# Layer two's weight pairs: sums in two parts, later roundings of what is stored, an earlier plan, and reused x tiles

## The chip, the core and the metric

The kernel runs on one core of one Trainium2 chip. The time is the device time of one execution in microseconds (us), taken over several executions; the profile is one further execution. The engines that matter here: TensorE (PE) multiplies matrices, ScalarE (ACT) and VectorE (DVE) work elementwise, SyncE (SP) and GpSimd (POOL) issue the transfers (DMAs). Each engine goes through its own instructions strictly in their order in the program; between engines semaphores hold an instruction back until what it reads is there, or until the memory that it writes has been read out.

## What is computed

```python
def reference(q, k, v, moe_w_in, moe_w_out, moe_alpha, moe2_w_in, moe2_w_out):
    x = retention(q, k, v)            # decayed causal attention, 2304 tokens x 512
    h = x @ moe_w_in                  # layer one, 512 -> 2048
    x = (np.maximum(h, 0) + moe_alpha * np.minimum(h, 0)) @ moe_w_out
    h = x @ moe2_w_in                 # layer two, 512 -> 2048
    return (h / (1 + np.exp(-1.702 * h))) @ moe2_w_out
```

The lines above are a shortening of the reference. Weights arrive as 64-bit floats, whose words the kernel reads as pairs of 32-bit integers and turns into float32 itself.

## The kernel before, in words

It has three stretches: attention (to about 80 us), layer one (to about 490 us) and layer two (to the end). Every float32 product is made of three passes of PE over rounded halves: each operand is split into a rounded high half (`copy`, L85, on ACT) and the rest as a low half (`sub`, L88, on DVE).

**Layer one** is 80 steps. A step is a chunk of tokens (512 columns, in one chunk 256) and one of 16 blocks of 128 hidden units. `mm1` (L403) makes the hidden block in 12 matmuls; `activate` does two Relu on ACT (L413, L414) and one operation on DVE (L415); `split` makes the high half on ACT (L85, gsf<-g) and the low half on DVE (L88, gsf<-g,gsf); `mm2` (L446) multiplies these gsf halves with the second weight in 12 matmuls. PE runs `mm1` of step i and then `mm2` of step i-2. Steps 32 to 47 and 64 to 79 are 512 wide, steps 48 to 63 are 256 wide. In between, `x_split` (x<-xf) rounds the next chunk's inputs.

**Layer two** uses a scheme with seven products in place of eight, so its weights go through sums and differences of quarters. It runs as units of 12 or 6 matmuls (L567).

**The weight pairs of layer two** are the work that the change moves. There are eight pairs j of second weight rows. Each has two halves e. For one half: `w_load`/`w_piece` (L112, issued by POOL, two DMAs of 512 KB into a tile raw0 or raw1), `w_abs` (L116, ACT, into a tile cv), `w_clamp` (L120, L123, DVE), `w_top` (L130, DVE), `w_low` (L137, DVE, the last reader of the raw tile). For the pair then: `sums1` and `sums2` (four `add` each on DVE, L474); `r_store` (five DMAs of SP, L181 to L185: three quarters and the four sums of `sums1`, to rg in memory, needed later by layer two's first product); `b_hi` (L85, ACT, rounds a quarter or a sum in its own place, so it may only run once r_store has read that place out); `b_lo` (L200, DVE); `b_store` (L206, L208 or L211, SP, to sg in memory). Blocks 0, 3 and 6 are quarters of the converted words (cv), blocks 1, 2, 4 and 5 are sums.

**The order** is written by a plan: `pair_words` gives each action a time; `tick` turns a time into a place in the steps, and the main loop emits what is due after `mm1` and before `activate`, or after `mm2` and before `split`. A plan's time only sets the place in each engine's order; an instruction starts when its engine comes to it and its inputs are there. The plan's two first numbers are the times of the two halves' conversion, the next two those of their loads.

**The end of layer one**: `x2_load` (L504, SP) fetches layer one's result in two parts k = 0 and 1 into tiles xr, `x2_step` makes sums, high and low halves from them for layer two, `r_load` (L542, SP) fetches the first weights of layer two, `r_split` rounds them.

Of the kernel before, what the change touches and what calls it, by code (L numbers as in the profile page):

```python
# [7 lines left out]
F32 = mybir.dt.float32  # L8
# [21 lines left out]
R, RN = 3, 384  # L30
# [9 lines left out]
def kernel(  # L40
# [18 lines left out]
    def pool(name, bufs, **kw):  # L59
        return ctx.enter_context(tc.tile_pool(name=name, bufs=bufs, **kw))  # L60
# [4 lines left out]
    xp = (pool("xp", 1), pool("xq", 1))  # L65
# [27 lines left out]
    def at(time, fn, *args):  # L93
        events.append((time, len(events), fn, args))
# [118 lines left out]
    def pair_words(j, t0, t1, l0, l1, slots, home):  # L213
        for e, (t, ld) in enumerate(((t0, l0), (t1, l1))):
            key = 2, 2 * j + e
            at(tick(ld), w_load, key, w2, slots[e])
            at(tick(ld) + 0.01, w_piece, key, w2, 1)
            for fn, d in ((w_abs, 0.0), (w_clamp, 1.6), (w_top, 3.0), (w_low, 4.4)):
                at(tick(t + d), fn, key)
        t = t1 + 6.2  # L220
        at(tick(t), sums1, j, home)
        at(tick(t + 0.9), r_store, j)
        at(tick(t + 1.5), sums2, j)
        for g, blocks in enumerate(((0, 3), (6, 1), (2, 4, 5))):
            for i in blocks:
                at(tick(t + 1.8 + 2.4 * g), b_hi, j, i)
                at(tick(t + 4.2 + 2.4 * g), b_lo, j, i)
                at(tick(t + 5.4 + 2.4 * g), b_store, j, i)


    ld, r_t, k_t, s_t, sc_t, av_t, xs_t = {}, {}, {}, {}, {}, {}, {}
# [239 lines left out]
    xt2, g2, ws, rw, tm, bank, xr = {}, {}, {}, {}, {}, {}, {}  # L471
# [21 lines left out]
    def x2_load(r, k):  # L493
        for h in range(2):
            if r:
                t = cvp.tile([128, 2, RN], F32, tag="cv", name="xr", bufs=2)
            else:
                t = xp[0].tile([128, 2, RN], F32, tag=f"x{2 * k + h}", name="xr")
            xr[k, h] = t
            f = t.rearrange("p c n -> p (c n)")  # L500
            for c, (c0, c1) in enumerate(CH):
                s0, s1 = max(c0, r * 2 * RN), min(c1, r * 2 * RN + 2 * RN)
                if s0 < s1:
                    nc.sync.dma_start(  # L504
                        out=f[:, s0 - r * 2 * RN:s1 - r * 2 * RN],
                        in_=x1[c][:, 2 * h + k, s0 - c0:s1 - c0],
                    )
# [22 lines left out]
    def x2_steps(k, t, step, gap):  # L530
        for i in range(7):
            for phase in range(3):
                at(t + step * i + gap * phase, x2_step, k, i, phase)
# [153 lines left out]
    for m, t in enumerate(pace):  # L687
        d = 0.75 if m < 3 else 0.5
# [12 lines left out]
    with tc.manual_schedule():  # L701
# [47 lines left out]
        n1 = base + n_s  # L749
        homes = {c: xp[c] for c in range(2)}  # L750
        for n, (_, c, m0, _) in enumerate(BLOCKS[N_FIRST:], 1):
            homes[c] = xp[n % 2]
            for k in range(NK):
                t = starts[c, m0] - (4 if n == 1 else 4.4) + 0.9 * k
# [8 lines left out]
        def tick(us):  # L763
            for begin, length in PAUSES:
                us += length if us >= begin else 0
            i = max(n for n in range(n_s) if begins[n] <= us)
            return base + i + (us - begins[i]) / (begins[i + 1] - begins[i])

        for j, plan in enumerate((
# [4 lines left out]
        )):  # L774
            pair_words(j, *plan)
        for k in range(2):
            at(n1 - 5.6 + 3.0 * k, x2_load, 0, k)
            x2_steps(k, n1 - 4.6 + 2.8 * k, 0.35, 0.5)
        for n in range(3):
            at(n1 - 1.5, r_load, n)  # L780
        for n in range(2):
# [24 lines left out]
        for r in range(R):  # L806
# [18 lines left out]
            if r + 1 < R:  # L825
                for n in range(3):
                    at(z + 2 * NU - 9.2, r_load, n)
                for k in range(2):
                    at(z + NU + 1 + 23 * k, x2_load, r + 1, k)
                    x2_steps(k, z + NU + 5.2 + 23 * k, 2.8, 0.9)  # L830
# [84 lines left out]
```

## Time and profile before

| | before |
|---|---|
| median of 3 runs | 846.1 us (845.58 to 847.55) |
| the profiled execution | 845.46 us |
| its span on the core | 843.7 us |
| mean granted TensorE clock | 0.993 of full speed |
| PE busy | 826.7 us, 98% of the span |
| DVE busy | 633.7 us, 75% |
| ACT busy | 458.5 us, 54% |

The span goes from the first to the last instruction on the core, and the profiled execution's time is 1.8 us longer than it. A difference of the kernels is read against the runs; where time lies is read in the trace of the profiled execution. PE's busy time counts a matmul that the trace shows, at whatever clock.

### The profile page before, as it was taken

The numbers are of one execution on the slowest core, as the hardware profiler recorded it, in microseconds if no ns is written. First come the engines' busy times: TensorE is split into PE (matmuls) and PEld (weight loads), VectorE is DVE, ScalarE is ACT, GpSimd is POOL, SyncE is SP. The second block draws the span as 40 slices with busy tenths as digits, with TensorE's granted clock in tenths as the row PEclk, the third lists the DMA queues.
The fourth block names the chain that finished last, engine by engine and source line by source line (L and its number), as shares of the span: only waits on it lengthen the run. The fifth ranks groups of instructions, "written<-read, shape, count | busy, mean of one in ns | idle before, by whom it ended". The sixth has DMA issues, their size and how long they took to land.

```text
span 843.7 us, 13989 instructions
## 1 busy us (share of the span) xinstructions
PE 826.7 (98%) x5132; PEld 753.0 (89%) x5132; DVE 633.7 (75%) x1128; ACT 458.5 (54%) x920; POOL 17.7 (2%) x36
## 2 busy tenths in 40 slices
PE   9999999999999998899999999999999999999998
PEld 8788888888888886698888899999999999999998
DVE  3997887687483776666768697789787699677875
ACT  5643664554353445445534676666566576566553
POOL 0000000000000010000010000000000000000000
PEclk9999999999999999999999999999999999999999
DMA  8985843455065465646656544598543877545872
GB/s 309 318 302 171 271 154 104 151 188 175 18 234 204 115 201 172 204 154 205 194 151 219 198 157 132 197 325 303 179 130 109 319 265 269 172 130 177 293 271 78
DMA packets 66100, 166.97 MB, mean 198 GB/s; under 512 B 7152, under 2 KB 33392, under 8 KB 60272
## 3 DMA queue, kind: packets, MB, share of 16 engines
q1 hardware_dynamic: 61424, 149.30, 51.8%
q0 software_dynamic: 4608, 16.78, 6.8%
q8 instruction: 40, 0.66, 0.3%
q14 instruction: 28, 0.23, 0.1%
HBM read 128.83 MB, written 37.22 MB: 197 GB/s over the span
## 4 chain that ended last, share of the span: by engine, by line
PE 55%; DMA 3%; DVE 2%; issue 1%; ACT 1%; SPq 0%; DVEq 0%; ACTq 0%
PE acc L567 23%; PE h L567 18%; PE acc L446 7%; PE h L403 6%; DMA rg<-sums 2%; DMA sg<-cv 1%; DMA sg<-sums 0%; DVE gsf L88 0%; ACT gsf L85 0%; DVE cv L130 0%; DVE sums L200 0%; DVE cv L120 0%; DVE g L415 0%; SPq L211 0%; DVE sums L474 0%
## 5 line engine op out<-in xcount | busy, mean ns | idle before, releaser
L446 PE MATMUL acc<-gsf,w 128*128 128x512 f32 (+1 forms) x960 | 214.6, 373 | 8.2 <-ACT gsf L85 7.1
L403 PE MATMUL h<-x,w 128*128 128x512 f32 (+1 forms) x960 | 212.2, 370 | 0.0
L446 PEld LDWEIGHTS acc<-gsf,w 128*128 128x128 f32 x960 | 170.3, 191 | 40.9 <-ACT gsf L85 8.1
L403 PEld LDWEIGHTS h<-x,w 128*128 128x128 f32 x960 | 169.8, 191 | 31.1 <-DVE w L88 0.8
L85 ACT ACTIVATE gsf<-g 128x384 fp32r<-128x384 f32 (+2 forms) x248 | 132.8, 543 | 104.3 <-DVE g L415 62.7
L88 DVE TENSOR_TENSOR gsf<-g,gsf 128x384 fp32r<-128x384 f32 (+2 forms) x248 | 141.6, 580 | 54.9 <-ACT gsf L85 54.4
L415 DVE SCALAR_TENSOR_TENSOR g<-h,nalpha_sb,g 128x512 f32<-128x512 f32 (+1 forms) x80 | 55.6, 695 | 77.0 <-ACT h L414 76.8
L567 PE MATMUL acc<-x,ws 128*128 128x384 f32 x552 | 106.8, 334 | 0.0
L567 PE MATMUL acc<-gsf,ws 128*128 128x384 f32 x576 | 101.3, 334 | 0.0
L567 PEld LDWEIGHTS acc<-gsf,ws 128*128 128x128 f32 x576 | 100.0, 188 | 0.0
L567 PEld LDWEIGHTS acc<-x,ws 128*128 128x128 f32 x552 | 96.7, 188 | 0.0
L567 PE MATMUL h<-x,ws 128*128 128x384 f32 x456 | 90.3, 334 | 0.0
L413 ACT ACTIVATE g<-h 128x512 f32<-128x512 f32 (+1 forms) x80 | 43.9, 549 | 73.3 <-PE h L403 73.3
L567 PEld LDWEIGHTS h<-x,ws 128*128 128x128 f32 x456 | 80.1, 188 | 0.1
L567 PE MATMUL h<-gsf,ws 128*128 128x384 f32 x432 | 76.6, 334 | 0.0
L567 PEld LDWEIGHTS h<-gsf,ws 128*128 128x128 f32 x432 | 75.0, 188 | 0.2 <-DVE gsf L88 0.2
L474 DVE TENSOR_TENSOR tm<-h,tm 128x384 f32<-128x384 f32 x73 | 40.5, 555 | 32.0 <-PE h L567 27.8
L88 DVE TENSOR_TENSOR ws<-rw,ws 128x512 fp32r<-128x512 f32 x96 | 57.0, 617 | 0.0
L474 DVE TENSOR_TENSOR g<-g,g 128x384 f32<-128x384 f32 x93 | 51.5, 554 | 0.7
L85 ACT ACTIVATE ws<-rw 128x512 fp32r<-128x512 f32 x96 | 49.8, 569 | 0.2 <-DMA rw<-rg 0.2
L414 ACT ACTIVATE h<-h 128x512 f32<-128x512 f32 (+1 forms) x80 | 43.9, 549 | 0.0
L116 ACT ACTIVATE cv<-raw 128x1024 f32<-128x1024 f32 x32 | 36.3, 1133 | 6.6 <-DMA raw<-in_w_dram 5.0
(73 smaller groups left out, 702.5 us busy)
## 6 DMA issues: line engine op xcount, KB each, us to landing
ws<-sg SPq DMA_DIRECT2D x42, 1024.0 KB, 6.2
raw<-in_w_dram SPq DMA_DIRECT2D x32, 512.0 KB, 4.9
raw<-in_w_dram POOLq DMA_DIRECT2D x32, 512.0 KB, 5.0
ld<-in_qkv_dram SPq DMA_DIRECT2D x15, 864.0 KB, 6.1
rw<-rg SPq DMA_DIRECT2D x24, 512.0 KB, 3.5
rw<-rg SPq DMA_DIRECT2D x24, 384.0 KB, 3.1
sg<-sums SPq DMA_DIRECT2D x40, 128.0 KB, 2.1
kts<-in_kn_dram SPq DMA_DIRECT2D x16, 256.0 KB, 6.3
```

What stands on the lines that cost most here:

```text
L85: return nc.scalar.activation(out=out, in_=in_, func=ACTF.Copy)
L88: return eng.tensor_tensor(out=out, in0=a, in1=b.bitcast(F32), op=ALU.subtract)
L116: nc.scalar.activation(out=cvs[key], in_=raws[key][:, :, 1].bitcast(F32), func=ACTF.Abs)
L403: nc.tensor.matmul(out=t, lhsT=w[:, cw, k * 128:k * 128 + 128], rhs=x[:, cx], start=(i == 0), stop=(i == 3 * NK - 1),)
L413: nc.scalar.activation(out=g, in_=t, func=ACTF.Relu)
L414: nc.scalar.activation(out=t, in_=t, func=ACTF.Relu, scale=-1.0)
L415: nc.vector.scalar_tensor_tensor(out=g, in0=t, scalar=nalpha_sb[:, m:m + 1], in1=g, op0=ALU.mult, op1=ALU.add)
L446: nc.tensor.matmul(out=acc[0][d], lhsT=w[:, cw, d * 128:d * 128 + 128], rhs=g[:, cx], start=(m == m0 and i == 0), stop=(m == m1 - 1 and i ...
L474: nc.vector.tensor_tensor(out=out, in0=x, in1=y, op=op)
L567: nc.tensor.matmul(out=out, lhsT=w(cw), rhs=x(cx), start=(start and n == 0), stop=True, skip_group_check=True,)
```

## The change

In `pair_words` the stores of `r_store` come 0.6 later after the sums begin and `sums2` 1.2 later, behind them. The four groups of roundings are now (0, 3), (6), (1, 2) and (4, 5), at 3.2, 5.0, 6.6 and 8.6 after the sums begin; before they were (0, 3), (6, 1) and (2, 4, 5) at 1.8, 4.2 and 6.6. The low halves follow 2.4 after, the stores 1.3 after these. The table of the eight pairs has other times, mostly earlier by 3 to 9. `x2_load` of part k = 1 takes the tiles that part 0 had (x0, x1) in place of two others, and is begun later, as are its steps.

```diff
@@ -219,13 +219,13 @@
                 at(tick(t + d), fn, key)
         t = t1 + 6.2
         at(tick(t), sums1, j, home)
-        at(tick(t + 0.9), r_store, j)
-        at(tick(t + 1.5), sums2, j)
-        for g, blocks in enumerate(((0, 3), (6, 1), (2, 4, 5))):
+        at(tick(t + 1.5), r_store, j)
+        at(tick(t + 2.7), sums2, j)
+        for d, blocks in ((3.2, (0, 3)), (5.0, (6,)), (6.6, (1, 2)), (8.6, (4, 5))):
             for i in blocks:
-                at(tick(t + 1.8 + 2.4 * g), b_hi, j, i)
-                at(tick(t + 4.2 + 2.4 * g), b_lo, j, i)
-                at(tick(t + 5.4 + 2.4 * g), b_store, j, i)
+                at(tick(t + d), b_hi, j, i)
+                at(tick(t + max(d + 2.4, 5.2)), b_lo, j, i)
+                at(tick(t + max(d + 2.4, 5.2) + 1.3), b_store, j, i)
 
 
     ld, r_t, k_t, s_t, sc_t, av_t, xs_t = {}, {}, {}, {}, {}, {}, {}
@@ -495,7 +495,7 @@
             if r:
                 t = cvp.tile([128, 2, RN], F32, tag="cv", name="xr", bufs=2)
             else:
-                t = xp[0].tile([128, 2, RN], F32, tag=f"x{2 * k + h}", name="xr")
+                t = xp[0].tile([128, 2, RN], F32, tag=f"x{h}", name="xr")
             xr[k, h] = t
             f = t.rearrange("p c n -> p (c n)")
             for c, (c0, c1) in enumerate(CH):
@@ -767,15 +767,15 @@
             return base + i + (us - begins[i]) / (begins[i + 1] - begins[i])
 
         for j, plan in enumerate((
-            (143, 158.5, 133, 151, (0, 0), 0), (186, 192.5, 178, 183, (0, 1), 2),
-            (206.5, 212.5, 194, 201, (0, 1), 2), (226.5, 232.5, 214.5, 221, (0, 1), 0),
-            (249, 260, 241, 251.8, (1, 0), 3), (274.5, 280.5, 257, 268.5, (1, 0), 1),
-            (296, 307, 289, 300, (0, 1), 2), (322, 328, 304.5, 316, (0, 1), 2),
+            (134, 149.5, 124, 141, (0, 0), 0), (178, 186, 171, 178, (0, 1), 2),
+            (201.5, 207.5, 186, 198.5, (0, 1), 2), (223, 229, 208, 220, (0, 1), 0),
+            (250.5, 259, 241.5, 250.8, (1, 0), 3), (274.5, 280.5, 258, 271.5, (1, 0), 1),
+            (301, 310, 293, 302, (0, 1), 2), (325.5, 331.5, 308, 322.5, (0, 1), 2),
         )):
             pair_words(j, *plan)
         for k in range(2):
-            at(n1 - 5.6 + 3.0 * k, x2_load, 0, k)
-            x2_steps(k, n1 - 4.6 + 2.8 * k, 0.35, 0.5)
+            at(n1 - 5.6 + 4.1 * k, x2_load, 0, k)
+            x2_steps(k, n1 - 4.7 + 4.0 * k, 0.3, 0.5)
         for n in range(3):
             at(n1 - 1.5, r_load, n)
         for n in range(2):
```

What that does to the engines' orders, at three places. First ACT around pair 2, from L414 of step 42 of the kernel before (cv are quarters of the pair, sums its sums; the L116 is the first half of pair 3):

```order
L414 ACTIVATE h<-h 128x512
L85 ACTIVATE cv<-cv 128x256 x2
L85 ACTIVATE gsf<-g 128x512
L85 ACTIVATE cv<-cv 128x256
L85 ACTIVATE sums<-sums 128x256
L413 ACTIVATE g<-h 128x512
L414 ACTIVATE h<-h 128x512
L85 ACTIVATE sums<-sums 128x256 x3
L116 ACTIVATE cv<-raw 128x1024
L85 ACTIVATE gsf<-g 128x512
```

The same place in the changed kernel, from the gsf of step 41 on:

```order
L85 ACTIVATE gsf<-g 128x512
L85 ACTIVATE cv<-cv 128x256 x2
L413 ACTIVATE g<-h 128x512
L414 ACTIVATE h<-h 128x512
L85 ACTIVATE cv<-cv 128x256
L85 ACTIVATE sums<-sums 128x256 x2
L85 ACTIVATE gsf<-g 128x512
L85 ACTIVATE sums<-sums 128x256 x2
L116 ACTIVATE cv<-raw 128x1024
L413 ACTIVATE g<-h 128x512
```

The first rounding of sums stood between gsf of step 42 and L413 of step 43; now two of them stand ahead of gsf of step 42, half a step earlier, and L116 stands ahead of L413 of step 43 instead of behind it.

Second, DVE around pair 3: the conversion of its second half, in the kernel before from L415 of step 45 on (x<-xf,x is an input half of a later chunk):

```order
L415 SCALAR_TENSOR_TENSOR g<-h,nalpha_sb,g 128x512
L130 SCALAR_TENSOR_TENSOR cv<-raw,cv 128x1024
L137 SCALAR_TENSOR_TENSOR cv<-raw,cv 128x1024
L88 TENSOR_TENSOR x<-xf,x 128x256
L88 TENSOR_TENSOR gsf<-g,gsf 128x512
L474 TENSOR_TENSOR sums<-cv 128x256
```

and in the changed kernel:

```order
L130 SCALAR_TENSOR_TENSOR cv<-raw,cv 128x1024
L88 TENSOR_TENSOR x<-xf,x 128x256
L88 TENSOR_TENSOR gsf<-g,gsf 128x512
L137 SCALAR_TENSOR_TENSOR cv<-raw,cv 128x1024
L415 SCALAR_TENSOR_TENSOR g<-h,nalpha_sb,g 128x512
L474 TENSOR_TENSOR sums<-cv 128x256
```

L130 and L137 stood behind L415 of step 45; L137 now ends just ahead of it, and the first sums follow L415 at once.

Third, ACT around the same pair, from L414 of step 46 on, before:

```order
L414 ACTIVATE h<-h 128x512
L85 ACTIVATE cv<-cv 128x256 x2
L85 ACTIVATE x<-xf 128x256
L85 ACTIVATE cv<-cv 128x256
L85 ACTIVATE sums<-sums 128x256
L85 ACTIVATE gsf<-g 128x512
L85 ACTIVATE sums<-sums 128x256 x3
```

and in the changed kernel from the quarters on:

```order
L85 ACTIVATE cv<-cv 128x256 x3
L413 ACTIVATE g<-h 128x512
L414 ACTIVATE h<-h 128x512
L85 ACTIVATE sums<-sums 128x256 x2
L85 ACTIVATE x<-xf 128x256
L85 ACTIVATE gsf<-g 128x512
L85 ACTIVATE sums<-sums 128x256 x2
```

The quarters are rounded ahead of L413 of step 46; a rounding of sums still stands ahead of gsf of step 46, now two of them and ahead of the x half too.

## Rows read from the trace of the kernel before

**Rows 1.** The page, part 1: engines' busy us, share of the span, instructions:

```profile
PE 826.7 (98%) x5132; PEld 753.0 (89%) x5132; DVE 633.7 (75%) x1128; ACT 458.5 (54%) x920; POOL 17.7 (2%) x36
```

**Rows 2.** Windows of 20 us; columns as in the first line:

```profile
core 0: us, PE busy (x) PEld busy (x) DVE busy (x) ACT busy (x) POOL busy (x), PEclk, DMA share, GB/s
...
320.00:340.00 20.00, 17.39 (x69) 13.58 (x68) 15.43 (x27) 10.28 (x20) 1.05 (x2) 0.91 0.44 137
340.00:360.00 20.00, 16.35 (x92) 14.04 (x91) 12.18 (x26) 9.96 (x24) 1.05 (x2) 0.91 0.70 223
...
380.00:400.00 20.00, 18.05 (x132) 17.30 (x132) 13.38 (x27) 10.63 (x27) 0.00 (x0) 0.91 0.64 212
```

**Rows 3.** PE's waits, 200 to 500 us: total us, times, longest:

```profile
PE acc L446 <- ACT gsf L85: 7.1, 3, 3.6
PE acc L446 <- DVE gsf L88: 1.1, 1, 1.1
```

**Rows 4.** PE's timeline: start us, us, instruction, count, [idle before <-releaser]:

```profile
320.34 2.88 PE L403 MATMUL h<-x,w 128*128 128x512 f32 x12
325.83 4.58 PE L446 MATMUL acc<-gsf,w 128*128 128x512 f32 x12 [2.61 <-ACT gsf L85]
...
333.28 2.88 PE L446 MATMUL acc<-gsf,w 128*128 128x512 f32 x12
...
341.44 1.73 PE L403 MATMUL h<-x,w 128*128 128x256 f32 x12
...
352.96 0.40 PE L446 MATMUL acc<-gsf,w 128*128 128x512 f32 x1
...
384.50 1.60 PE L403 MATMUL h<-x,w 128*128 128x256 f32 x12
...
400.42 2.90 PE L403 MATMUL h<-x,w 128*128 128x512 f32 x12
```

**Rows 5.** One window of 2 us after the first gap, columns as rows 2:

```profile
328.00:330.00 2.00, 2.00 (x6) 1.52 (x5) 1.97 (x4) 0.13 (x1) 0.00 (x0) 0.50 0.83 285
```

**Rows 6.** ACT's timeline where it waited:

```profile
321.32 0.42 ACT L85 ACTIVATE sums<-sums 128x256 fp32r<-128x256 f32 x1 [4.46 <-issue]
...
324.14 1.12 ACT L116 ACTIVATE cv<-raw 128x1024 f32<-128x1024 f32 x1 [0.33 <-DMA sg<-cv]
...
345.83 0.42 ACT L85 ACTIVATE sums<-sums 128x256 fp32r<-128x256 f32 x1 [3.36 <-DMA rg<-sums]
...
384.08 0.42 ACT L85 ACTIVATE sums<-sums 128x256 fp32r<-128x256 f32 x1 [3.54 <-DMA rg<-sums]
```

**Rows 7.** DVE's timeline: w_low of pairs 2, 3, 4; then two later places:

```profile
310.80 1.22 DVE L137 SCALAR_TENSOR_TENSOR cv<-raw,cv 128x1024 int32<-128x1024 int32 x1
...
336.32 1.23 DVE L137 SCALAR_TENSOR_TENSOR cv<-raw,cv 128x1024 int32<-128x1024 int32 x1
...
374.50 1.22 DVE L137 SCALAR_TENSOR_TENSOR cv<-raw,cv 128x1024 int32<-128x1024 int32 x1
...
394.28 0.42 DVE L88 TENSOR_TENSOR gsf<-g,gsf 128x256 fp32r<-128x256 f32 x1
...
478.85 1.02 DVE L88 TENSOR_TENSOR x<-xr,x 128x384 fp32r<-128x384 f32 x2
```

**Rows 8.** POOL's timeline: loads of pair 3's two halves:

```profile
307.57 1.56 POOL L112 DMA_DIRECT2D raw<-in_w_dram  x2 [17.73 <-issue]
312.56 1.05 POOL L112 DMA_DIRECT2D raw<-in_w_dram  x2 [3.42 <-issue]
```

**Rows 9.** Line L184, first stored sums of the eight pairs, issue to landing:

```profile
DMA to landing us min/median/max: 2.0/6.5/7.6
```

**Rows 10.** Timelines of SP and PE at the end of layer one:

```profile
474.03 1.75 SPq L504 DMA_DIRECT2D xr<-x  x4
...
490.40 6.77 PE L567 MATMUL h<-x,ws 128*128 128x384 f32 x38
```

**Rows 11.** Line L542, 460 to 500 us, from issue to landing:

```profile
DMA to landing us min/median/max: 3.1/5.5/6.7
```

**Rows 12.** The page, part 6: POOL's raw loads, KB each, median us to landing:

```profile
raw<-in_w_dram POOLq DMA_DIRECT2D x32, 512.0 KB, 5.0
```

## The prediction

> **What bounds the kernel now.** I read the page's busy times first, then the twenty-microsecond windows, then what TensorE (PE) waited for. PE is busy 98% of the span [rows 1]. From 160 to 500 us PE is busy for all of every 20 us, except in three windows [rows 2], and the list of PE's waits holds only two entries, both for gsf, the two rounded halves of layer one's activations [rows 3]. So only those places can give time back; DVE or ACT work made quicker elsewhere gives nothing.
>
> What a place costs I take from PE's starts [rows 4]. A 512-wide step is two groups of 12 matmuls at 2.72 us, a 256-wide one two at 1.44 us (the differences of starts where nothing waits).
> - Site 1: three groups after 320.34 the next should start at 328.50 and starts at 333.28: 4.78 us lost.
> - Site 2: after 341.44 come groups of 1.44, 2.72 and 1.44; the next, due at 347.04, starts at 352.96: 5.92 us.
> - Site 3: eight groups of 1.44 after 384.50 end at 396.02; the next starts at 400.42: 4.40 us.
>
> Together 15.1 us. Part of each is TensorE's clock: after each gap the granted clock falls to 0.50 (1.2 of 2.4 GHz), for which one of three such windows stands [rows 5], and the group after the first gap takes 4.58 instead of 2.88 us [rows 4]: about 1.7 us a site.
>
> Why PE waits: ACT is in order, and at each site its rounding of the first stored sums (L85, sums<-sums) stands ahead of a gsf rounding. It waits 4.46, 3.36 and 3.54 us for the store of those sums (rg<-sums, L184) to land [rows 6]; the first row names no releaser, the two others name the store. The store is late because of a raw load. POOL issues the next load into a raw tile as soon as w_low (L137) has read it: L137 ends at 312.02, the load starts at 312.56 [rows 7, 8]. Its 1 MB is under way when SP comes to the sums' store; these stores take 2.0 us from issue at best, 6.5 in the median and 7.6 at worst [rows 9]. With W the end of the second half's w_low (312.02, 337.55, 375.72 [rows 7]) the waits end at W+9.3, W+8.3 and W+8.4 [rows 6].
>
> **The change part by part.** It takes no arithmetic out; instructions move. My frame is the steps of before with the stalls taken out: times up to 323 are those of before, at sites 2 and 3 PE's times in the frame are 4.78 earlier up to 341, and at site 3 I stay in before's own clock times.
>
> *The loads.* Their times in the table change, but a load waits for w_low whatever its plan says, and their order on POOL is the same. So I keep W+8.3 to W+9.3 for the landing. By the Trainium skill, "DMA: Bandwidth & Descriptors", section "Queues, rings and completion order", each DMA engine takes turns between the rows of queues that have work, a packet at a time, so that a store shares with a load and need not wait it out. The trace's 6.5 us in the median against 2.0 at best shows more delay than sharing alone would lead me to expect; by that rule the stores would land some 3 us sooner and all three sites would be clear, 831, which is a rival below.
>
> *The roundings.* The first stored sums are planned 2.4 us later after the sums begin (6.6 instead of 4.2). Waits of 3.4 to 4.5 us thus become 1 to 2 by plan. What stands behind them on ACT decides what PE sees.
>
> *Pair 2 (site 1).* Its conversions come a step (5.44 us) sooner, so W is 312.02−5.44 = 306.6 at the latest; at the earliest 304.5, if DVE, which in before came to them late, has 2 us less ahead of it. The store lands from 304.5+8.3 = 312.8 to 306.6+9.3 = 315.9. Two roundings of sums now stand ahead of gsf of step 42: 0.33+0.33+0.62 gives 314.1 to 317.2. PE takes that gsf one group before 320.34, at 317.62: no stall. Behind it on ACT stands w_abs of pair 3 (1.12 us), which writes a tile that quarter stores must have left; in before it started 2.8 after the sums' rounding [rows 6]. L413, L414 and the next gsf queue behind it, L415 and DVE's clamps too: gsf's low half of step 43 is ready at 321.8 to 323.9, wanted at 323.5 (the group's 323.06 and two matmuls), that of step 44 at 327.7 to 329.8, wanted at 329.0. Left over 0 to 0.8; I take 0.4.
>
> *Pair 3 (site 2).* Here the plan goes only 3.5 sooner. L137 moves ahead of L415 of step 45, which takes W from 332.8 (337.55 less the 4.78) to between 328.8 and 331.0. Landing at +8.3: 337.1 to 339.3. On ACT two roundings, one of the next x and gsf follow, 1.6 us: 338.7 to 340.9, wanted at 338.1 (323.06 and 5.44+5.44+2.72+1.44). Left over 0.6 to 2.8; I take 1.6. No row tells whether the clock falls after so short a wait: the shortest that it followed in before are site 3's, of about 1 us each, two in a row [rows 3]. I take no fall, and a fall of 1.7 as the upper end.
>
> *Pair 4 (site 3).* W moves about 1 us forward, the landing to 383.0, and the roundings stand behind L413 and L414 of step 58, so that its gsf is there at 384.1, wanted at 385.9: that wait is gone. Left is DVE, which has the same four L200, the x halves and two clamps ahead of L415 of step 60. In before the low half of step 60 ended at 394.70 [rows 7]; 1.1 sooner by the landing and 0.8 by L413 and L414 (with L415 behind them) no longer waiting, it ends at 392.8, wanted at 391.9 (384.50+5×1.44+0.24). I take 0.9, from 0 to 2.6.
>
> *Other pairs.* They have no stall before. Pair 1: W 281.3, landing at 290.0, gsf of step 38 at 291.3, wanted at 295.86 (320.34−2.72−4×5.44): 4.5 spare. Pair 0 meets no load. Pairs 5 to 7 round later than now and move by 3 to 5 at most; I cost them at nothing, covered by the gsf buffers' two steps, and at 1 us each, 3 together, if that cover is gone (part of the range's upper end).
>
> *End of layer one.* x2_load of k=1 reuses the tiles of k=0 and so waits for k=0's last readers on DVE, which end at 479.87 in before [rows 7], where the load was issued at 474.03 [rows 10]. SP is in order, so the three weight loads behind it move by the same 5 to 6 us, to about 481; from issue to landing such loads take 6.7 at the slowest [rows 11], 488. Layer two's first matmul comes at 490.40 [rows 10]: covered. DVE's low halves for the first units fit with about 0.3 us to spare. I take 0.25, from 0 to 0.5.
>
> Sum: 0.4+1.6+0.9+0.25 = 3.2 of 15.1 stay, 11.9 go. Of the profiled run's 845.46 us (its span is 843.7) this leaves 833.6; the median of the runs, 846.1, is 0.64 above it, so 834.2.
>
> **The rivals.**
> *Late at pair 3.* W_3 at the late end: 2.8 us and a fall of the clock, 4.5 in place of 1.6, makes 837.1; site 1 and site 3 at their upper ends add 2.1, the cover of pairs 5 to 7 part of 3: up to 841. For it: pair 3 has the smallest shift. Against: DVE has to be at its slowest.
> *Nothing left.* The stores land 2 or 3 us sooner than W+8.3, and all 15.1 go: 831.0, with 0.5 either way. For it: the best landing of 2.0 [rows 9]. Against: the three sites' landings after W agree within 1 us, and each has its load just ahead, as the changed plan has.
> *Not begun sooner.* The conversions wait for tiles that the pair before frees (w_abs as at 324.14 [rows 6]), so W_2 stays, and ACT's wait only changes place, from ahead of L413 to ahead of gsf: 312.02+9.3 and 1.3 more is 322.6 against 317.62, 5.0 at site 1, as before. It decides from W_2 past 308. Then 843 to 846. Against: the stores of pair 1 move ahead with pair 1, by 8 in the plan.
> *Slower: two loads ahead of the stores.* If the w_low of a pair's two halves come closer together, the second load is issued while the first is under way, and the stores queue behind 2 MB. A raw load takes 5.0 us from issue to landing in the median [rows 12]; a further delay D of up to that costs 3D over the sites and three falls of the clock: 3.2+5.1+3D. From D = 2.8 that passes the 15.1 us by 0.2%; at D = 4, 851.4. Against: in before the load of 307.57 started 5 us before that of 312.56 [rows 8], and its landing was W+9.3 instead of W+8.3, a D of 1.
>
> **How the numbers follow.** A measurement here can tell about 0.2% (1.7 us) from no change. Forecast, 832 to 836.5: 0.48. Late at pair 3, 836.5 to 841: 0.22. Nothing left, 830.5 to 832: 0.16. Not begun sooner: 0.06, two thirds of it within 0.2%. Slower: 0.08. Faster is 0.48+0.22+0.16+0.02 = 0.88, same 0.04, slower 0.08. The range goes from nothing left (830.5) to late at pair 3 with all upper ends (841) and holds some 0.83.
>
> **What would show it.** In the changed profile: PE's windows from 300 to 400 nearly full; its waits for ACT's gsf under 2 us, the longest near step 46; ACT's sums<-sums waiting 1 to 2 us for rg<-sums; one dip of the clock or none; landings of rg<-sums still over 6 us after issue; at the end of layer one the weight loads issued 5 us later and no wait at L567. I am wrong if the sums' store lands past W+10, if ACT waits as long as before but ahead of gsf, or if a unit of layer two waits for x2.

## The result, and the profile after

The changed kernel takes 834.15 us in the median of 4 runs (832.85 to 834.64), the kernel before 846.67 us in the runs beside it (4 runs, 845.58 to 847.55): a ratio of 0.9849 with a 95% interval of 0.9831 to 0.9868, 12.5 us less. Measured again it gave 833.23 against 845.47 (0.9859, 0.9836 to 0.9882). The forecast was 834.2.

PE's waits between 200 and 500 us in the changed kernel (total us, times, longest), which answer to [rows 3]:

```profile
PE h L403 <- ACT x L85: 1.1, 1, 1.1
PE acc L446 <- DVE gsf L88: 0.3, 1, 0.3
```

The wait for ACT's gsf, 7.1 us in three places, is gone; what is left is one wait of a new kind (an input half x) and a fraction of a microsecond for a low half. The windows of 20 us that answer to [rows 2], same columns:

```profile
320.00:340.00 20.00, 18.86 (x87) 15.20 (x86) 16.72 (x32) 9.37 (x22) 1.05 (x2) 1.00 0.55 172
340.00:360.00 20.00, 20.00 (x144) 18.67 (x144) 13.39 (x26) 11.07 (x27) 2.10 (x4) 1.00 0.58 177
...
380.00:400.00 20.00, 19.67 (x128) 17.79 (x128) 18.29 (x35) 10.35 (x24) 1.05 (x2) 1.00 0.51 153
```

PE is idle for 1.1 and 0.3 us where it was idle for 2.6, 3.7 and 2.0, and the granted clock stays at 1.00 (2.4 GHz) in all three, where it was 0.91. PE's timeline at what is left of the three sites, as [rows 4]:

```profile
320.45 2.88 PE L403 MATMUL h<-x,w 128*128 128x512 f32 x12
...
331.58 2.88 PE L403 MATMUL h<-x,w 128*128 128x512 f32 x12
...
337.02 1.23 PE L403 MATMUL h<-x,w 128*128 128x256 f32 x9
339.31 0.96 PE L403 MATMUL h<-x,w 128*128 128x256 f32 x3 [1.06 <-ACT x L85]
340.12 3.17 PE L446 MATMUL acc<-gsf,w 128*128 128x512 f32 x12
343.12 1.59 PE L403 MATMUL h<-x,w 128*128 128x256 f32 x12
...
383.30 0.40 PE L446 MATMUL acc<-gsf,w 128*128 128x256 f32 x2
384.02 1.46 PE L446 MATMUL acc<-gsf,w 128*128 128x256 f32 x10 [0.33 <-DVE gsf L88]
385.32 1.60 PE L403 MATMUL h<-x,w 128*128 128x256 f32 x12
```

With the pitches of before (2.72 and 1.44): at site 1 four groups after 320.45 should end at 331.33, the next starts at 331.58, 0.25 lost. At site 2 the groups after 337.02 should start at 338.46 and 341.18 and start at 340.12 and 343.12, 1.94 lost. At site 3 one group after 383.30 starts at 385.32 instead of 384.74, 0.58 lost. That is 2.8 us where it was 15.1.

The chain that the prediction followed, in the new rows: DVE's w_low of pairs 2 and 3 with one L415 between them, POOL's load, and ACT's waits with pair 3's first w_abs (L116).

```profile
304.03 1.23 DVE L137 SCALAR_TENSOR_TENSOR cv<-raw,cv 128x1024 int32<-128x1024 int32 x1
...
318.96 0.75 DVE L415 SCALAR_TENSOR_TENSOR g<-h,nalpha_sb,g 128x512 f32<-128x512 f32 x1 [1.25 <-ACT h L414]
...
329.02 1.22 DVE L137 SCALAR_TENSOR_TENSOR cv<-raw,cv 128x1024 int32<-128x1024 int32 x1
```

```profile
305.80 1.05 POOL L112 DMA_DIRECT2D raw<-in_w_dram  x2 [3.42 <-issue]
```

```profile
315.06 0.73 ACT L85 ACTIVATE sums<-sums 128x256 fp32r<-128x256 f32 x2 [3.88 <-issue]
315.69 0.62 ACT L85 ACTIVATE gsf<-g 128x512 fp32r<-128x512 f32 x1
...
316.82 1.12 ACT L116 ACTIVATE cv<-raw 128x1024 f32<-128x1024 f32 x1
...
338.23 0.72 ACT L85 ACTIVATE sums<-sums 128x256 fp32r<-128x256 f32 x2 [1.76 <-DMA rg<-sums]
338.86 0.40 ACT L85 ACTIVATE x<-xf 128x256 fp32r<-128x256 f32 x1
339.17 0.61 ACT L85 ACTIVATE gsf<-g 128x512 fp32r<-128x512 f32 x1
...
374.21 0.73 ACT L85 ACTIVATE sums<-sums 128x256 fp32r<-128x256 f32 x2 [1.52 <-DMA rg<-sums]
```

W, the end of w_low, is 305.26 and 330.24; the load follows 0.54 behind, as before; the waits end at W+9.8 and W+8.0 (before W+9.3 and W+8.3 [rows 6, 7]). So the stores land as late as ever, and ACT still waits 3.9 us at pair 2. What changed is what stands behind: gsf of step 42 is there at 316.3 and is asked for at 317.73. The wait does reach pair 3, though: behind it on ACT stand w_abs of pair 3 and L413 and L414 of step 43; DVE's L415 waits for that L414 until 318.96, and from there to the end of pair 3's w_low at 330.24 DVE has no gap. That the stores come no sooner is what L184's landings say too, 6.6 us in the median where it was 6.5 [rows 9]:

```profile
DMA to landing us min/median/max: 3.0/6.6/8.1
```

The end of layer one, SP's and PE's timelines, against [rows 10]. The first L567 stands at 478.23, 12.2 us earlier; x2_load of part 1 is issued 11.7 us before it, where it was 16.4:

```profile
466.51 1.92 SPq L504 DMA_DIRECT2D xr<-x  x4
468.48 9.13 SPq L542 DMA_DIRECT2D rw<-rg  x4
```

```profile
478.23 7.83 PE L567 MATMUL h<-x,ws 128*128 128x384 f32 x42
485.90 1.20 PE L567 MATMUL acc<-x,ws 128*128 128x384 f32 x6
```

The 42 matmuls take 7.67 us to the next start; the kernel before took 7.30 from 490.40 (its next unit starts at 497.70). So 0.4 us are lost at layer two's start that were not lost before.

### The profile page after: what moved, and what is told of

Its sections match the earlier page's. It is cut to its first block, busy times and chain, and to the rows that moved or that the text cites. A ratio compares the mean times of both kernels' runs of the same rounds, so it can differ in the third digit from the quotient of the medians.

```text
span 832.9 us, 13984 instructions
## 1 busy us (share of the span) xinstructions
PE 820.6 (99%) x5132; PEld 747.6 (90%) x5132; DVE 633.6 (76%) x1128; ACT 458.7 (55%) x920; POOL 18.1 (2%) x36
## 4 chain that ended last, share of the span: by engine, by line
PE 75%; DVE 10%; DMA 8%; ACT 3%; issue 2%; SPq 1%; DVEq 0%; ACTq 0%
PE acc L567 22%; PE h L567 18%; PE h L403 16%; PE acc L446 15%; DMA rg<-sums 2%; PE av L271 2%; DVE cv L137 1%; DVE cv L130 1%; DMA xr<-x 1%; DMA rg<-cv 1%; DVE gsf L88 1%; DVE cv L120 1%; DMA raw<-in_w_dram 1%; PE st L271 1%; PE sc L271 1%
## 5 line engine op out<-in xcount | busy, mean ns | idle before, releaser
L446 PE MATMUL acc<-gsf,w 128*128 128x512 f32 (+1 forms) x960 | 210.6, 368 | 0.3 <-DVE gsf L88 0.3
L446 PEld LDWEIGHTS acc<-gsf,w 128*128 128x128 f32 x960 | 168.1, 188 | 31.3 <-DVE gsf L88 1.3
L415 DVE SCALAR_TENSOR_TENSOR g<-h,nalpha_sb,g 128x512 f32<-128x512 f32 (+1 forms) x80 | 55.6, 695 | 68.1 <-ACT h L414 67.8
L567 PE MATMUL acc<-x,ws 128*128 128x384 f32 x552 | 106.8, 334 | 0.0
L567 PE MATMUL acc<-gsf,ws 128*128 128x384 f32 x576 | 101.3, 334 | 0.0
L567 PEld LDWEIGHTS acc<-gsf,ws 128*128 128x128 f32 x576 | 100.0, 188 | 0.0
L567 PEld LDWEIGHTS acc<-x,ws 128*128 128x128 f32 x552 | 96.7, 188 | 0.0
L567 PE MATMUL h<-x,ws 128*128 128x384 f32 x456 | 90.6, 334 | 0.1
L413 ACT ACTIVATE g<-h 128x512 f32<-128x512 f32 (+1 forms) x80 | 43.9, 549 | 71.9 <-PE h L403 71.7
L567 PEld LDWEIGHTS h<-x,ws 128*128 128x128 f32 x456 | 80.1, 188 | 0.5 <-DVE x L88 0.4
L567 PE MATMUL h<-gsf,ws 128*128 128x384 f32 x432 | 77.2, 335 | 0.4 <-ACT gsf L85 0.3
L567 PEld LDWEIGHTS h<-gsf,ws 128*128 128x128 f32 x432 | 74.9, 188 | 1.3 <-DVE gsf L88 0.8
L414 ACT ACTIVATE h<-h 128x512 f32<-128x512 f32 (+1 forms) x80 | 44.0, 549 | 0.0
L116 ACT ACTIVATE cv<-raw 128x1024 f32<-128x1024 f32 x32 | 36.2, 1132 | 8.5 <-DVE cv L137 3.4
```

Of the source, the lines that this page charges most:

```text
L116: nc.scalar.activation(out=cvs[key], in_=raws[key][:, :, 1].bitcast(F32), func=ACTF.Abs)
L413: nc.scalar.activation(out=g, in_=t, func=ACTF.Relu)
L414: nc.scalar.activation(out=t, in_=t, func=ACTF.Relu, scale=-1.0)
L415: nc.vector.scalar_tensor_tensor(out=g, in0=t, scalar=nalpha_sb[:, m:m + 1], in1=g, op0=ALU.mult, op1=ALU.add)
L446: nc.tensor.matmul(out=acc[0][d], lhsT=w[:, cw, d * 128:d * 128 + 128], rhs=g[:, cx], start=(m == m0 and i == 0), stop=(m == m1 - 1 and i ...
L567: nc.tensor.matmul(out=out, lhsT=w(cw), rhs=x(cx), start=(start and n == 0), stop=True, skip_group_check=True,)
```

## Experiments

What a program lost in layer one is worked out in the same way in each trace: starts of PE's groups, less the pitches. What is lost is put to the pair of weights whose chain held PE up. It is one execution each; the times are medians of 4 to 10 runs.

| program | site 1 | site 2 | site 3 | layer two's start | median us |
|---|---|---|---|---|---|
| before | 4.8 | 5.9 | 4.4 | 0.0 | 845.5 to 846.7 |
| changed | 0.2 | 1.9 | 0.6 | 0.4 | 834.2 |
| changed, again | 0.0 | 0.3 | 0.5 | 0.2 | 833.2 |
| table alone | 0.0 | 4.4 | 2.4 | 0.0 | 837.8 |
| order in a pair alone | 7.0 | 2.3 | 6.3 | 0.0 | 844.8 |
| before, loads by SP | 3.3 | 1.7 | 2.9 | 0.0 | 839.9 |
| changed, loads by SP | 0.0 | 0.0 | 2.2 | 0.3 | 833.1 |
| changed, old x2_load | 0.0 | 0.9 | 0.6 | 0.0 | 832.5 |
| changed, pair 3 later | 0.0 | 0.0 | 0.6 | 0.3 | 831.4 |
| changed, pairs 3 and 5 later | 0.0 | 0.0 | 1.7 | 0.0 | 832.3 |
| SP loads, pair 5 later, old x2_load | 0.0 | 0.0 | 0.9 | 0.0 | 832.0 |
| changed, pair 3 later, old x2_load | 0.0 | 0.0 | 0.5 | 0.0 | 831.7 |

Beside the first four experiments the kernel before gave 845.7, beside the next four 845.8 and beside the last two 845.5; executions of one program differ by 1 to 5 us.

**The table alone.** The kernel before with the changed table of the eight pairs. By it pairs 0 to 3 convert 3.5 to 9 earlier; pairs 4 to 7 lie between 1 earlier and 5 later:

```diff
-            (143, 158.5, 133, 151, (0, 0), 0), (186, 192.5, 178, 183, (0, 1), 2),
-            (206.5, 212.5, 194, 201, (0, 1), 2), (226.5, 232.5, 214.5, 221, (0, 1), 0),
+            (134, 149.5, 124, 141, (0, 0), 0), (178, 186, 171, 178, (0, 1), 2),
+            (201.5, 207.5, 186, 198.5, (0, 1), 2), (223, 229, 208, 220, (0, 1), 0),
...
```

> The kernel before with the changed table of the eight pairs alone; order of sums, stores and roundings within a pair, and x2_load, as before. Theory (earlier pairs and later roundings each do a part; the sums' store still lands 8 to 10 us after w_low): pair 2 rounds its first sum ahead of L413 of step 42, lands near 314.8, gsf of step 42 about 318 against 317.7, so site 1 keeps 0.5 to 1.5 us; pair 3 rounds it ahead of L413 of step 46, so L413, L414, L415 and gsf follow a landing near 338.2 and gsf is there near 341 against 338.5, site 2 keeps 2.7 to 4.5; site 3 keeps 0.6 to 1. Together 5 to 6.5 of 15.1: 837 (836 to 839). Rival, the earlier table does it all: 834. Rival, the later roundings do it all: 845 to 847.

Measured: 837.8 us, ratio 0.9900 (0.9874 to 0.9925). The theory's 837 holds. ACT's timeline at pair 3 shows the term that it keeps:

```profile
337.24 0.42 ACT L85 ACTIVATE sums<-sums 128x256 fp32r<-128x256 f32 x1 [3.17 <-DMA rg<-sums]
337.56 0.58 ACT L413 ACTIVATE g<-h 128x512 f32<-128x512 f32 x1
...
339.47 0.40 ACT L85 ACTIVATE x<-xf 128x256 fp32r<-128x256 f32 x1
339.78 0.62 ACT L85 ACTIVATE gsf<-g 128x512 fp32r<-128x512 f32 x1
```

The wait is 3.2 us again, and L413, L414, three more roundings and x stand between it and gsf; PE stops first, for 1.8 us, for that x half. The sum came out, its parts less so: site 1 loses nothing (0.5 to 1.5 expected), site 2 4.4 and site 3 2.4 (0.6 to 1 expected).

**The order within a pair alone.** Table and x2_load of before, with this:

```diff
-        at(tick(t + 0.9), r_store, j)
-        at(tick(t + 1.5), sums2, j)
-        for g, blocks in enumerate(((0, 3), (6, 1), (2, 4, 5))):
+        at(tick(t + 1.5), r_store, j)
+        at(tick(t + 2.7), sums2, j)
+        for d, blocks in ((3.2, (0, 3)), (5.0, (6,)), (6.6, (1, 2)), (8.6, (4, 5))):
...
```

> The kernel before with the changed order within a pair alone (stores, second sums and roundings), table and x2_load as before. Theory: site 1 stays at 4.8 or a little more, since w_abs of pair 3 stands ahead of gsf of step 43 on ACT and still waits for the quarter stores to land near 324; site 2 falls to 1 to 1.7, since the sums are rounded behind gsf of step 46; site 3 to 1 to 2.5. Together about 9 of 15.1: 840.5 (838.5 to 843). Rival, the later roundings do it all: 834 to 836. Rival, the earlier table does it all: 845 to 847.

Measured: 844.8 us, ratio 1.0000 (0.9985 to 1.0016): nothing gained. The theory said 840.5, and missed. ACT's timeline at site 1:

```profile
325.20 0.72 ACT L85 ACTIVATE sums<-sums 128x256 fp32r<-128x256 f32 x2 [4.73 <-issue]
326.85 1.12 ACT L116 ACTIVATE cv<-raw 128x1024 f32<-128x1024 f32 x1 [0.94 <-DMA sg<-cv]
327.87 0.62 ACT L85 ACTIVATE gsf<-g 128x512 fp32r<-128x512 f32 x1
```

The later roundings wait 4.7 us too, since the store is still beside the load (ACT's wait ends 10.6 us after pair 2's w_low, which itself ends at 314.58, 2.6 us later than in the kernel before). w_abs, which waits for quarter stores that the new order also puts later, then waits 0.9 us more ahead of gsf: site 1 loses 7.0, not 4.8. At site 3 6.3 us are lost, not 4.4: w_abs waits 1.6 us (the profile names a load of xf), and the last sums' roundings now stand between it and gsf. Together that eats up the 3.6 us won at site 2. ACT's timeline at site 3:

```profile
388.84 1.12 ACT L116 ACTIVATE cv<-raw 128x1024 f32<-128x1024 f32 x1 [1.55 <-DMA xf<-x]
389.86 0.71 ACT L85 ACTIVATE sums<-sums 128x256 fp32r<-128x256 f32 x2
390.47 0.40 ACT L85 ACTIVATE gsf<-g 128x256 fp32r<-128x256 f32 x1
```

So the order alone is worth nothing; behind the earlier table it is worth 6.8 less 2.8, some 4 us in layer one.

**The loads issued by SP**, so that a second half's load stands behind the sums' stores in the same queue, in the changed kernel and in the one before:

```diff
-        eng = nc.sync if key[0] == 1 else nc.gpsimd
+        eng = nc.sync
```

> The changed kernel with the raw loads of layer two's weights issued by SP in the plan's order, so that the second half's load stands behind the sums' stores in SP's queue and not beside them. Theory (the load is what makes the sums' store slow): rg<-sums lands 2 to 3.5 us after issue instead of 6.6, ACT no longer waits for it, site 2 falls from 1.9 to 0.3 or less: 832 (831.5 to 833.5); quarter stores, now behind the load, may land later, and keep 0.3 to 1 at site 1. Rival, the store is slow by itself (its many small pieces): landings stay at 6 to 7 us and the time at 834.

> The kernel before with the raw loads issued by SP in the plan's order, so that second halves' loads stand behind the sums' stores; nothing else changed. Theory (load delays store, and that alone makes ACT wait ahead of gsf): rg<-sums lands in 2 to 3.5 us and ACT's three waits of 3.4 to 4.5 us are gone; site 2 falls from 5.9 to 0.5 or less, site 3 from 4.4 to about 1 (DVE), site 1 keeps up to 4.8 if w_abs still waits for quarter stores that now queue behind the load: 838 (832 to 840). Rival, the store is slow by itself: 845 to 847.

Measured: 833.1 us (0.9853, 0.9829 to 0.9877) and 839.9 us (0.9928, 0.9911 to 0.9944). L184's landings, first in the changed kernel, then in the one before:

```profile
DMA to landing us min/median/max: 2.0/2.0/3.9
```

```profile
DMA to landing us min/median/max: 2.0/2.1/2.2
```

From 6.6 and 6.5 us to 2.0 and 2.1, with the same stores: the load is the cause, and the rival of a store slow by itself is out. (The load left POOL's queue and came behind the stores in one move; which of the two does it is not separated.) ACT no longer waits for rg<-sums anywhere, and that takes 5.8 us from the kernel before. Its trace loses 7.2 us less, of which some 5 are the three falls of the clock, for the granted clock is 1.00 throughout. But site 2 keeps 1.7 us and site 3 2.9, where the theory had 0.5 and 1: w_abs, which ACT now reaches sooner, waits ahead of gsf for quarter stores that stand behind the loads (the 256 KB ones land 4.0 us after issue in the median, where it was 2.5; those of 128 KB 4.0, where it was 4.2). ACT's waits in the kernel before with SP's loads (260 to 470 us), and its timeline at site 3 of the changed one:

```profile
ACT cv L116 <- DMA sg<-cv: 12.4, 5, 4.2
```

```profile
376.36 1.15 ACT L116 ACTIVATE cv<-raw 128x1024 f32<-128x1024 f32 x1 [2.18 <-DMA sg<-cv]
377.41 0.40 ACT L85 ACTIVATE gsf<-g 128x256 fp32r<-128x256 f32 x1
```

In the changed kernel sites 1 and 2 lose nothing and site 3 loses 2.2 instead of 0.6: the time is that of the changed kernel within the measurement.

**The old x2_load** in the changed kernel:

```diff
-                t = xp[0].tile([128, 2, RN], F32, tag=f"x{h}", name="xr")
+                t = xp[0].tile([128, 2, RN], F32, tag=f"x{2 * k + h}", name="xr")
...
-            at(n1 - 5.6 + 4.1 * k, x2_load, 0, k)
-            x2_steps(k, n1 - 4.7 + 4.0 * k, 0.3, 0.5)
+            at(n1 - 5.6 + 3.0 * k, x2_load, 0, k)
+            x2_steps(k, n1 - 4.6 + 2.8 * k, 0.35, 0.5)
```

> The changed kernel with the loads and steps of layer two's inputs (x2_load, x2_steps) as before: own tiles for part 1, begun earlier. Theory: it gives the 0.4 us back that units of layer two wait at their start, and nothing else; 833.8 (833 to 835). Rival, why the change moved it: the own tiles hold the last pair's sums, which now leave later, so SP stands at this load, the weight loads behind it come late, and layer two starts 1 to 3 us late: 835 to 837.

Measured: 832.5 us, 0.9849 (0.9827 to 0.9871). SP issues the second x2_load at 463.85, 1.3 us after the last sums' store, and the weight loads right behind:

```profile
458.08 4.51 SPq L211 DMA_DIRECT2D sg<-sums  x8
463.85 1.75 SPq L504 DMA_DIRECT2D xr<-x  x4
465.64 1.38 SPq L542 DMA_DIRECT2D rw<-rg  x3
```

Layer two starts without its 0.4 us. The rival's delay does not show: the reuse of the tiles costs what the prediction gave it, and this trace shows no need for it. The time is below the range expected, and this execution lost 0.9 us at site 2, not 1.9, which the theory did not count on. This program differs from the one with the table alone only in the order within a pair: 0.9849 against 0.9900, intervals apart, so behind the earlier table that order is worth some 4.3 us by the times too.

**Pair 3's sums later**, behind the x half and gsf of step 46, and **pair 5's conversions later** in addition:

```diff
-        for d, blocks in ((3.2, (0, 3)), (5.0, (6,)), (6.6, (1, 2)), (8.6, (4, 5))):
+        for d, blocks in ((3.2, (0, 3)), (5.0, (6,)), (8.0 if j == 3 else 6.6, (1, 2)), (8.6, (4, 5))):
```

```diff
-            (250.5, 259, 241.5, 250.8, (1, 0), 3), (274.5, 280.5, 258, 271.5, (1, 0), 1),
+            (250.5, 259, 241.5, 250.8, (1, 0), 3), (276.5, 281.5, 258, 271.5, (1, 0), 1),
```

> The changed kernel with one more move: pair 3's first sums are rounded at 8.0 instead of 6.6 after the sums begin, which puts them behind the x half and gsf of step 46 on ACT. Theory (what is left at site 2 is ACT standing for the sums' store ahead of the x half and gsf): site 2 falls from 1.9 us to 0.3 or less, the first matmul group of step 48 starts on time; 832.5 (832 to 833.5). Rival, the wait only moves on to L413 of step 47 and gsf of step 47: 1 us stays, 833.5 to 834.5.

> As the run before, and pair 5's conversions 2.0 and 1.0 us later in the table, which puts w_abs behind gsf of step 59 and x, and the clamps behind gsf of step 60. Theory (what is left at site 3 is DVE's clamps and ACT's w_abs ahead of gsf): site 3 falls from 0.6 to 0.2 or less; 832 (831.3 to 833). Rival: the clamps are late for the next step instead, 0.5 to 1 us stays.

Measured: 831.4 us (0.9837, 0.9816 to 0.9858) and 832.3 us (0.9847, 0.9826 to 0.9868). In the first, ACT's timeline at pair 3 has gsf ahead of the wait, and site 2 loses nothing, although the sums' store lands 1.0 us after step 48 has begun (339.45), much as in the changed kernel (338.23 against 337.02):

```profile
339.32 0.63 ACT L85 ACTIVATE gsf<-g 128x512 fp32r<-128x512 f32 x1 [0.48 <-DVE g L415]
340.48 1.50 ACT L85 ACTIVATE sums<-sums 128x256 fp32r<-128x256 f32 x4 [0.53 <-DMA rg<-sums]
```

In the second, the rival came true, though not by the clamps: step 60 is in time, step 61 loses 1.7, because ACT's x half waits for a tile that pair 4's sums' stores have not left yet, and gsf stands behind it:

```profile
382.55 0.63 ACT L85 ACTIVATE x<-xf 128x512 fp32r<-128x512 f32 x1 [3.77 <-DMA sg<-sums]
383.09 0.40 ACT L85 ACTIVATE gsf<-g 128x256 fp32r<-128x256 f32 x1
```

**Two combinations**: SP's loads with pair 5 later and the old x2_load; and pair 3 later with the old x2_load, beside the changed kernel itself.

> The changed kernel with the raw loads issued by SP, pair 5's conversions 2.0 and 1.0 us later, and x2_load and its steps as before. Theory: with the sums' store quick, sites 1 and 2 lose nothing, site 3 (2.2 us in the run with SP's loads, w_abs waiting for quarter stores ahead of gsf) falls to 0.5 or less, layer two starts without its 0.4: 831.5 (830.5 to 832.5), the lowest of all. Rival: w_abs waits as long behind gsf and delays the steps after, 1 to 2 us stay: 832.5 to 833.5.

> The changed kernel with pair 3's first sums rounded at 8.0 instead of 6.6 and with x2_load and its steps as before: the two moves that each took a leftover away, together. Theory (the leftovers are independent: 1.9 us at site 2, 0.4 at layer two's start; site 3 keeps 0.6): what is lost in layer one and at layer two's start falls from 3.2 to about 0.7 us; by the median 2.5 below the changed kernel of the same chip: 831.5 (830.5 to 832.5). Rival: executions differ by more than that in attention and in layer two's second half, and no difference to the changed kernel shows.

> The changed kernel itself once more, on the same chip as the run before it, to compare the two medians: 833.9 (833 to 835) by the first measurement.

Measured: 832.0 us (0.9839, 0.9818 to 0.9860), 831.7 us (0.9845, 0.9828 to 0.9862) and 833.2 us (0.9859, 0.9836 to 0.9882). In the first, site 3 keeps 0.9 us where the theory had 0.5 or less, and it is not the lowest of all. In the second, PE's only wait from 200 to 500 us is

```profile
PE acc L446 <- DVE gsf L88: 0.3, 1, 0.3
```

and layer one loses 0.5 us. Its median is 1.5 below the changed kernel's on the same chip, but the intervals overlap: that it is the faster is likely by its trace and not settled by its time. The changed kernel's second execution lost only 0.3 at site 2, where the first lost 1.9:

```profile
327.31 1.22 DVE L137 SCALAR_TENSOR_TENSOR cv<-raw,cv 128x1024 int32<-128x1024 int32 x1
```

```profile
336.44 0.72 ACT L85 ACTIVATE sums<-sums 128x256 fp32r<-128x256 f32 x2 [1.68 <-DMA rg<-sums]
```

W is 328.53 instead of 330.24, the landing W+7.9: W is 1.7 us sooner and 1.7 us less are lost, as the prediction's range for pair 3 had it. W itself follows ACT's wait at pair 2, which ends at 313.06 instead of 315.06:

```profile
313.06 0.73 ACT L85 ACTIVATE sums<-sums 128x256 fp32r<-128x256 f32 x2 [2.62 <-issue]
...
315.10 1.14 ACT L116 ACTIVATE cv<-raw 128x1024 f32<-128x1024 f32 x1 [0.18 <-DVE gsf L88]
```

From the start of pair 3's first w_abs to W it is 13.4 us in both executions (316.82 to 330.24, 315.10 to 328.53), and 13.4 again in the two programs with SP's loads and the changed table (314.62 to 328.03, 316.78 to 330.19). So the time at which ACT comes to pair 3's first w_abs decides when pair 3's load and stores begin, and with them what site 2 loses; in the changed kernel the wait for pair 2's sums sets that time. This is read from the traces, and no experiment moved that wait alone.

## Why the prediction was right, point by point

- **The three sites are all there is.** 15.1 us lost before; 2.8 and 0.4 after in one trace, 0.8 and 0.2 in the other; no other group of PE in layer one loses more than 0.1 us from 160 us on, so pairs 0, 1 and 5 to 7 cost nothing, as assumed. The medians moved by 12.5 and 12.2. The forecast's 11.9 was right to half a microsecond, partly by luck, since the leftover differs by 2 us between two executions. The first profiled execution itself is only 10.8 us below that of before (834.64 against 845.46), since it loses 1.1 us more in layer two (last section).
- **The load delays the store.** Shown by the SP runs. The landing after w_low stayed at W+7.9 to W+9.8 in the changed kernel, with the load beside the store, and went to W+3.5 with it behind.
- **Site 1: 0.4 forecast, 0.2 and 0.0 measured.** W_2 was to be between 304.5 and 306.6 and was 305.26 and 304.53. The wait on ACT is not 1 to 2 us, as the plan's times had it, but 3.9 and 2.6: the step that was off. Its price at site 1 was right because it was put on what is behind, not on the wait. But the prediction, which saw w_abs and DVE's clamps queue behind this wait, did not carry it on to pair 3.
- **Site 2: 1.6 forecast, 1.9 and 0.3 measured.** W_3 was to be 328.8 to 331.0, from the order on DVE alone, and was 330.24 and 328.53, set by the wait at pair 2. The cause of the spread was not foreseen, and it is luck that the first trace lies near the middle of the range. The step also named the wrong victim: PE first waited for the x half in the first group of step 48 (due 1.1 us into it), which stands ahead of gsf on ACT; gsf came in its shadow. The time was the same, since both stand behind the same rounding.
- **Site 3: 0.9 forecast, 0.6 and 0.5 measured**, DVE's queue as said; the fall of the clock that the upper end had did not come.
- **The clock**: none of the gaps left (1.66 us at most) was followed by a fall; 1.00 in every window. In the run with the table alone, site 2's 2.4 us was followed by one (the group after it took 4.50 instead of 2.88 us). The three falls of before, 1.7 us each, were some 5 of the 12 us.
- **Layer two's start: 0.25 forecast, 0.4 and 0.2 measured.** No wait for the weights, as said; a low half of the inputs was late (in the first trace DVE ends it at 480.34, and PE's next matmul starts at 480.39).
- **The reading of the skill's rule was off.** The prediction took sharing between queues to mean a store some 3 us sooner, and the 6.5 us as evidence against it. The changed kernel's trace shows sharing: of the transfers issued between 304 and 316 us (KB each, median us to landing) the load beside the stores takes 7.6 where the median is 5.0 [rows 12], and the sums' stores 8.2, so that the stores land only a little after the load:

```profile
raw<-in_w_dram POOLq DMA_DIRECT2D x2, 512.0 KB, 7.6
rg<-sums SPq DMA_DIRECT2D x2, 256.0 KB, 8.2
```

  In the Trainium skill, "DMA: Bandwidth & Descriptors", section "Queues, rings and completion order", engines take turns between queues, and this agrees: both are slowed. What was wrong was the size that the prediction drew from it, and with it the "nothing left" rival, whose stores never landed sooner. It left out that the sums' stores stand behind 384 KB of quarters in their own queue: 896 KB of stores that share evenly with a load of 1,024 KB would end near its end (an estimate from the sizes, not tested by itself).
- **The rivals.** "Late at pair 3" is what the first trace is near (1.9 of 2.8) and the second is not. "Not begun sooner" and "two loads ahead" did not occur: W_2 moved by 6.8 us, and the halves' loads are 5.0 us apart (300.81 and 305.80). The latter's 851.4 adds up to 851.3.

## What to carry to other kernels

A wait on an in-order engine costs what stands behind it, not its length: here a wait of 1.8 us cost 1.9, and one of 3.9 us did not delay the gsf behind it. But what stands behind it has to be followed to its end: the wait of 3.9 us also held back the next pair's conversion, and where it ended 2.0 us sooner, the next site lost 1.7 us less. So first look at what a stalled instruction has queued behind it, on its own engine and on those that this engine feeds, and move the urgent one ahead, before shortening the wait. Two moves that look separate can be worth nothing alone (the later roundings) and 4 us together with the one that makes room for them; test each alone and each taken away.

## What was not expected of the hardware

A store next to a load is slower, and the load too: 256 KB beside a 1 MB load land 6.5 us after issue, alone or ahead of it 2.0. Putting the load behind the stores in one queue makes the sums' stores fast, but the waits moved from the sums' rounding to w_abs, which waits for the quarter stores behind the load (12.4 us in five places in the kernel before).

Executions of one program differ by 1 to 5 us, and much of it lies outside the part that was changed. In the traces of these programs step 16 of layer one starts between 162.3 and 165.4 us, ahead of all that was moved. In layer two's next round an input load (xr) landed late enough to stop gsf in the changed kernel's first execution (1.1 us lost around 548 us) and in some others, and in its second not at all:

```profile
546.70 0.53 ACT L85 ACTIVATE x<-xr 128x384 fp32r<-128x384 f32 x1 [4.09 <-DMA xr<-x]
```

What decides whether that load is late was not tried, nor why pair 2's stores land 9.8 us after W in one execution of the changed kernel and 8.5 in the other.
